# An adaLN attention block on one core: the third tile's mean on two engines, and the shift in two column halves

## The chip, the core and the metric

The kernel runs on one core of a Trainium2 chip. A core has a matrix engine (TensorE, PE in the profile; its weight loads are the row PEld), a vector engine (VectorE, DVE), a scalar engine (ScalarE, ACT), a general engine (GpSimd, POOL) and a sync engine (SyncE, SP) that here issues nearly all DMA transfers. Each engine works through its own queue of instructions in order, and waits on semaphores for the others. Working data lie in SBUF, results of matrix products in the eight banks of PSUM. The metric is the device time of one execution in microseconds, the median of several runs.

## The reference

```python
B, N, D = (2, 256, 1152)
mod = (_silu(c) @ w_mod).reshape(B, 6, 1, D)
shift_a, scale_a, gate_a, shift_m, scale_m, gate_m = [mod[:, i] for i in range(6)]
h = _layernorm(x, axis=-1) * (1 + scale_a) + shift_a
qkv = h @ wqkv
q, k, v = (qkv[..., :D].copy(), qkv[..., D:2 * D].copy(), qkv[..., 2 * D:].copy())
p = _softmax(jnp.einsum('bqd,bkd->bqk', q, k) * D ** (-0.5), axis=-1)
a = jnp.einsum('bqk,bkd->bqd', p, v) @ wo
return x + gate_a * a
```

All inputs are bf16. wqkv is 1152 x 3456, wo 1152 x 1152, w_mod 1152 x 6912, of which only the columns of shift_a, scale_a and gate_a are used.

## The kernel before, in words

The 512 tokens (two batches of 256) are four token tiles of 128; the width of 1152 is nine blocks of 128. `tok(b)` is a batch's tokens, `one(t)` a tile's. Every instruction is recorded by a helper class, so all of them have line 85 in the profile, and `pin` (line 98) fixes each engine's order to the order of the program text. The order of the text is therefore the schedule of every queue, SP's loads among them.

**Loads.** SP issues x's tiles 0 to 2, the columns of `scale_a` for blocks 0 and 1 (`load_s(PA, ...)`), K's first row of weight blocks (`load_k(0, 1)`), x's tile 3 (line 175), K's second row (line 176), and then the other scale columns in parts PB, PC, PD (blocks 2 to 4, 5 and 6, 7 and 8) between K's rows. Behind K come the columns of `shift_a` into wH (line 190, three loads by rows), Q's rows (line 192), the gate's columns into wG (lines 542 to 545), V and wo.

**The start.** Eleven matmuls on junk data keep PE going (`fillers`, line 362). A token tile's mean is formed by DVE statistics (tile 0), by an ACT pass with an accumulated sum (tiles 1 and 2, `act_mean`), or by ACT over 640 columns and DVE over 512, the two sums joined on DVE (tile 3, lines 402 to 405). `centre` subtracts it on DVE (xc), PE transposes the nine blocks (tp in PSUM), and DVE and ACT copy them to xcT. The division by the standard deviation comes later (`normalised`, with rstd spread over the tokens).

**Scale.** For blocks 0 and 1, `scale_open` writes ones into a bank with a one-row matmul, and `scale_rows` adds the product of silu(c) and the weights, so the bank holds 1 + scale. For PB, `scale_tiles` (line 297) computes the product in four column groups of PE side by side, with 32 rows of output each, and `scale_turned` transposes 32 x 32 squares on DVE into sT and adds 1 into s1p. `scaled` and `scaled_tp` multiply xcT or tp by it: hTs, the input of K.

**K.** Five of K's nine column blocks accumulate in five banks (`accs`) over the nine rows: `k_part` for rows 0 and 1, batch 0, tile 2 and tile 3 apart, since they arrive apart; `k_step` for the other rows with all 512 tokens. The remaining four column blocks are done for rows 0 and 1 in pairs (`pair_part`, bank psE), put away in `held` (`park`), and finished later by `held_block` (bank psK) with `add_held`. PSUM is five banks in a ring (MM) and three single ones (BA, BB, BC); a new use of a bank waits until its last reader is done.

**Shift.** `shift_tiles` (line 502) multiplies silu(c) by wH, in four column groups again, into psH; `shift_turned` transposes it to shT, and `shifted(i)` adds it to hT, block by block and batch by batch, every third on ACT. Then nine rows of Q follow (five accumulators, then four more blocks), then scores, V, attention times V, and wo with the gate. The gate is formed on DVE meanwhile, in 18 multiply-adds over wG's rows (`gate_steps`), and summed over partitions on POOL.

Of the kernel before, what the change touches and what calls it, by code (L numbers as in the profile page):

```python
# [16 lines left out]
def kernel(  # L17
# [10 lines left out]
    P = 128  # L28
# [37 lines left out]
    def bank(shape, name, dtype=None, where=None):  # L66
        if where is None:
            where = ring[turn_no[0] % len(ring)]
            turn_no[0] += 1
        return where[0].tile(shape, dtype or F32, tag=where[1], name=name)  # L70
# [36 lines left out]
    def tok(b):  # L107
        return slice(b * N, (b + 1) * N)

    def one(t):  # L110
        return slice(t * P, (t + 1) * P)
# [25 lines left out]
    ones_row = const.tile([1, 2 * NR], BF16)  # L137
# [10 lines left out]
    def load_x(t):  # L148
        spq.dma_start(out=x_sb[:, t, :], in_=x_f[t * P : (t + 1) * P, :])

    def load_mod(tile_, which, k0, k1, c0, c1):
        spq.dma_start(out=tile_[:, k0:k1, c0:c1], in_=wmod_v[:, k0:k1, which, c0:c1])
# [4 lines left out]
    def load_k(k0, k1, c0=0, c1=D):  # L157
        spq.dma_start(out=wK[:, k0:k1, c0:c1], in_=wqkv_v[:, k0:k1, D + c0 : D + c1])

    def load_q(k0, k1):  # L160
        spq.dma_start(out=wQ[:, k0:k1, :], in_=wqkv_v[:, k0:k1, 0:D])
# [12 lines left out]
    load_k(0, 1)  # L174
    load_x(3)
    load_k(1, 2)
# [12 lines left out]
    for k0, k1 in ((0, 4), (4, 8), (8, KT)):  # L189
        load_mod(wH, 0, k0, k1, 0, D)  # L190
    for k0, k1 in ((0, 1), (1, 3), (3, 5), (5, 7)):
        load_q(k0, k1)

# [28 lines left out]
    ssum3 = small.tile([P, 1], F32, tag="ssum", name="ssum")  # L222
# [12 lines left out]
    def act_mean(t):  # L235
        sca.activation(out=xc[:, t, :], in_=x_sb[:, t, :], func=ACT.Copy, scale=-1.0 / D,
                       accum_out=nmean[:, t : t + 1])

# [4 lines left out]
    def centre(t, scalar, op, c0=0, c1=D):  # L243
        vec.tensor_scalar(out=xc[:, t, c0:c1], in0=x_sb[:, t, c0:c1], scalar1=scalar, scalar2=None, op0=op)
# [4 lines left out]
    def transposes(t, h, where):  # L249
        k0, k1 = HALF[h]  # L250
        tp = bank([P, 5, P], "tp", BF16, where)
        for k in range(k0, k1):
            ten.transpose(tp[:, k - k0, :], xc[:, t, k * P : (k + 1) * P], ident)
        tps[t, h] = tp

    def xcT_copy(t, h, on_dve, skip=0):
        k0, k1 = HALF[h]
        dst, srct = xcT[:, k0 + skip : k1, one(t)], tps[t, h][:, skip : k1 - k0, :]
        if on_dve:
            vec.tensor_copy(out=dst, in_=srct)  # L260
        else:
            sca.copy(out=dst, in_=srct)

# [33 lines left out]
    def scale_tiles(part, where):  # L297
        psS[part] = bank([P, part[1] - part[0], 32], "psS", where=where)
        for kk in range(KT):
            for j in range(4):  # L300
                ten.matmul(psS[part][32 * j : 32 * j + 32], lhsT=sc_rhs(kk), rhs=wS_v[:, kk, part[0] : part[1], j, :],
                           start=(kk == 0), stop=(kk == KT - 1))

    def scale_turned(part):
        vec.transpose(out=sT[:, part[0] : part[1], :].rearrange("p k c -> p (k c)"),
                      in_=psS[part].rearrange("p k c -> p (k c)"))
        vec.tensor_scalar_add(out=s1p[:, part[0] : part[1], :], in0=sT[:, part[0] : part[1], 0:B], scalar1=1.0)

    def scaled(k, sl, scalar):
        vec.tensor_scalar(out=hTs[:, k, sl], in0=xcT[:, k, sl], scalar1=scalar, scalar2=None, op0=ALU.mult)  # L310

    def scaled_tp(k, t):
        vec.tensor_scalar(out=hTs[:, k, one(t)], in0=tps[t, 0][:, k, :], scalar1=s1p[:, k, t // NQ : t // NQ + 1],
                          scalar2=None, op0=ALU.mult)

    def scaled_b(k, b):
        scaled(k, tok(b), s1p[:, k, b : b + 1])
# [52 lines left out]
    act_mean(2)  # L370
    gps.tensor_scalar_mul(out=snm[:, 1:3], in0=nmean[:, 1:3], scalar1=float(D) ** -0.5)
    transposes(0, 0, MM)
    transposes(0, 1, MM)
    xcT_copy(0, 0, True)
    xcT_copy(0, 1, False)
    transposes(1, 0, MM)
    transposes(1, 1, MM)
    scale_rows(PA, 0, 4)
    xcT_copy(1, 0, True)
    centre(2, nmean[:, 2:3], ALU.add)  # L380
    xcT_copy(1, 1, False)
    scale_rows(PA, 4, KT, js=[(0, 1), (1, 2)])
    scaled(0, tok(0), psS[PA][:, 0, 0:1])
    vec.tensor_copy(out=s1p[:, PA[0] : PA[1], :], in_=psS[PA][:, :, 0:B])
    transposes(2, 0, BB)
    transposes(2, 1, BC)
    scaled_tp(0, 2)
    scaled_b(1, 0)
    scaled_tp(1, 2)
    xcT_copy(2, 0, True, skip=KA)  # L390
    xcT_copy(2, 1, False)
# [3 lines left out]
    k_part(0, tok(0))  # L395
    k_part(0, one(2))
    pr20 = pair(1, 0, BA)
    pair_part(pr20, 0)
    pr10 = pair(0, 0, BC)
    pair_part(pr10, 0)  # L400
    H3, C3 = 5 * P, 4 * P
    sca.activation(out=xc[:, 3, 0:H3], in_=x_sb[:, 3, 0:H3], func=ACT.Copy, accum_out=ssum3)
    half3 = small.tile([P, 1], F32, tag="half3", name="half3")
    vec.reduce_sum(out=half3, in_=x_sb[:, 3, H3:D], axis=AX.X)
    vec.tensor_scalar(out=nmean[:, 3:4], in0=half3, scalar1=ssum3, scalar2=-1.0 / D, op0=ALU.add, op1=ALU.mult)
    centre(3, nmean[:, 3:4], ALU.add, 0, C3)
    centre(3, nmean[:, 3:4], ALU.add, C3, D)
    pair_part(pr10, 1)
    k_part(1, tok(0))
    k_part(1, one(2))  # L410
    park(pr10)
    transposes(3, 0, BB)
    pair_part(pr20, 1)
    transposes(3, 1, BC)
    scaled_tp(0, 3)
    scaled_tp(1, 3)
    xcT_copy(3, 0, True, skip=KA)
    park(pr20)
# [4 lines left out]
    k_part(0, one(3))  # L423
    scale_tiles(PB, BB)
    k_part(1, one(3))
    scale_turned(PB)
    for k in range(*PB):
        for b in range(B):
            scaled_b(k, b)
# [35 lines left out]
    held_block(1, PB, BC)  # L465
    pT3 = bank([P, P], "pT3", BF16, BB)
# [3 lines left out]
    k_step(5)  # L470
# [28 lines left out]
    psH = bank([P, KT, 32], "psH", where=BA)  # L499
    wH_v = wH.rearrange("p kk (k j c) -> p kk k j c", k=KT, j=4)  # L500

    def shift_tiles(kk0, kk1):
        for kk in range(kk0, kk1):
            for j in range(4):
                ten.matmul(psH[32 * j : 32 * j + 32], lhsT=sc_rhs(kk), rhs=wH_v[:, kk, :, j, :],
                           start=(kk == 0), stop=(kk == KT - 1))

    held_block(3, (KA, KA + 2), BC)
    shift_tiles(0, KT)
# [3 lines left out]
    def shift_turned(k0, k1):  # L513
        vec.transpose(out=shT[:, k0:k1, :].rearrange("p k c -> p (k c)"),
                      in_=psH[:, k0:k1, :].rearrange("p k c -> p (k c)"))
# [10 lines left out]
    shift_turned(0, 3)  # L526
    for i in range(KT * B):
        if i == B:
            shift_turned(3, KT)
        if i in (3 * B, 5 * B):  # L530
            normalised(KT - 2 if i == 3 * B else KT - 1)
        shifted(i)
    for i in (2, 3):
        add_held(i)
# [7 lines left out]
    load_mod(wG, 2, 0, 3, 0, D)  # L542
    load_q(7, KT)
    load_mod(wG, 2, 3, 6, 0, D)
    load_mod(wG, 2, 6, KT, 0, D)
# [6 lines left out]
    gates = [(b, kt) for g in range(0, KT, 3) for b in range(B) for kt in range(g, g + 3)]  # L552
# [15 lines left out]
    for k in range(KT):  # L568
        for f in range(QACC):
            ten.matmul(q_acc[f], lhsT=wq(k, f), rhs=hT[:, k, :], start=(k == 0), stop=(k == KT - 1))  # L570
# [177 lines left out]
```

## Time and profile before

The median of three runs is 95.64 us (95.59 to 95.98).

| | |
|---|---|
| profiled execution, its own time | 95.63 us |
| its span in the profile | 93.9 us |
| PE busy | 89.2 us, 95% of the span, 664 matmuls |
| DVE busy | 69.6 us, 74% |
| ACT busy | 33.9 us, 36% |
| POOL busy | 20.8 us, 22% |
| granted TensorE clock | 1.00 |
| read from HBM | 19.76 MB |
| first transposes / first K product / first Q product start | 6.47 / 8.95 / 30.26 us |

Times in the timelines count from the span's start. "x36" is the number of instructions in a line, and the duration ahead of it runs from the start of the first to the modelled end of the last. A matmul's end is modelled, so one can begin before the one ahead of it has ended. What stands in brackets is idle time of the engine before the line and what ended it. `SPq` lines are the issues of DMA transfers; the last number of a line in the list of transfers is the time from issue to landing.

### The profile page before, as it was taken

How to read it: one execution, taken by the hardware profiler on the slowest of the kernel's cores; microseconds unless marked ns; L12 is line 12 of the kernel's file. 1: busy time of each engine (PE TensorE's matmuls, PEld its weight loads, DVE VectorE, ACT ScalarE, POOL GpSimd, SP SyncE). 2: the span in 40 equal slices, each digit the busy share in tenths (PEclk: the TensorE clock that was granted, in tenths of full speed). 3: DMA queues.
4: the chain of work that ended last, by engine and by line, in shares of the span. 5: the costliest groups of instructions: out<-in, count | busy, mean ns of one | idle time of the engine just before them, and what ended most of it. 6: DMA issues, size and time to landing. Idle time of an engine off the chain costs nothing.

```text
span 93.9 us, 1692 instructions
## 1 busy us (share of the span) xinstructions
PE 89.2 (95%) x664; PEld 52.8 (56%) x664; DVE 69.6 (74%) x134; ACT 33.9 (36%) x69; POOL 20.8 (22%) x26
## 2 busy tenths in 40 slices
PE   3999999999999999999999999999999999999970
PEld 1348884545445444444478665656578665665660
DVE  2478789245997977999999899990028587888880
ACT  5188788002643600284220687324246200000010
POOL 5623000800000000000000000008999990002000
PEclk9999999999999999999999999999999999999999
DMA  2999999999999999999999702200000000312212
GB/s 23 345 282 374 372 397 362 369 410 407 407 405 410 414 408 412 402 373 365 381 407 410 296 17 56 63 0 0 0 0 0 0 0 8 125 42 83 114 45 92
DMA packets 17232, 21.31 MB, mean 227 GB/s; under 512 B 2249, under 2 KB 10569, under 8 KB 17225
## 3 DMA queue, kind: packets, MB, share of 16 engines
q1 hardware_dynamic: 16809, 21.17, 62.3%
q8 instruction: 5, 0.08, 0.3%
q10 hardware_dynamic: 416, 0.04, 0.3%
q14 instruction: 2, 0.02, 0.0%
HBM read 19.76 MB, written 1.18 MB: 223 GB/s over the span
## 4 chain that ended last, share of the span: by engine, by line
PE 91%; DVE 4%; issue 1%
PE ps L85 39%; PE psQ L85 19%; PE acc L85 11%; PE psK L85 7%; PE junk_ps L85 5%; PE s_ps L85 4%; PE tp L85 2%; PE psE L85 2%; PE psS L85 2%; DVE o_sb L85 2%; DVE ga L85 2%; PE psH L85 1%; DVE xc L85 1%; DVE junk L85 1%; PE bc_ps L85 0%
## 5 line engine op out<-in xcount | busy, mean ns | idle before, releaser
L85 POOL PARTITION_ALL_REDUCE gate_bc<-gacc x2 | 13.7, 6886 | 44.6 <-DVE gacc L85 44.6
L85 DVE SCALAR_TENSOR_TENSOR gacc<-wG,scT_f,gacc 128x1152 f32<-128x1152 bf16 x16 | 22.4, 1416 | 0.4
L85 PE MATMUL ps<-wV,hT 128*128 128x384 bf16 x108 | 17.7, 326 | 0.0
L85 PE MATMUL psQ<-hT,wQ 128*128 128x512 bf16 x81 | 17.6, 379 | 0.0
L85 PE MATMUL ps<-wO,attnT 128*128 128x384 bf16 (+3 forms) x108 | 17.2, 322 | 0.0
L85 PEld LDWEIGHTS <-attnT 128*128 128x128 bf16 x117 | 11.1, 98 | 6.5
L85 PEld LDWEIGHTS <-hT 128*128 128x128 bf16 x108 | 10.6, 98 | 6.9
L85 PEld LDWEIGHTS <-wK 128*128 128x128 bf16 x109 | 9.5, 97 | 6.9 <-issue 0.2
L85 PEld LDWEIGHTS <-wQ 128*128 128x128 bf16 x81 | 7.9, 98 | 9.6
L85 PE MATMUL acc<-hTs,wK 128*128 128x512 bf16 (+2 forms) x65 | 11.2, 314 | 0.0
L85 DVE TENSOR_TENSOR ga<-ps,gate_bc 128x384 f32<-128x384 f32 (+3 forms) x12 | 6.5, 545 | 3.0 <-PE ps L85 3.0
L85 ACT CAST qkT<-psQ 128x512 bf16<-128x512 f32 x9 | 4.9, 597 | 10.6 <-PE psQ L85 10.6
L85 DVE CAST attnT<-ps 128x512 bf16<-128x512 f32 (+1 forms) x6 | 3.5, 603 | 6.8 <-PE ps L85 6.8
L85 ACT CAST v_sb<-ps 128x384 bf16<-128x384 f32 x12 | 5.5, 476 | 7.9 <-PE ps L85 7.9
L85 PE MATMUL psK<-hTs,wK 128*128 128x512 bf16 x28 | 7.0, 379 | 0.0
L85 DVE TENSOR_TENSOR o_sb<-ga,x_sb 128x384 bf16<-128x384 f32 (+3 forms) x12 | 6.6, 548 | 0.4
L85 ACT CAST o_sb<-ps 128x128 bf16<-128x128 f32 x1 | 0.3, 265 | 17.3 <-PE ps L85 17.3
L85 PE MATMUL junk_ps<-junk 128*128 128x512 bf16 x11 | 4.9, 629 | 1.5 <-DVE junk L85 1.5
L85 DVE TENSOR_TENSOR hT<-hTs,held 128x512 bf16<-128x512 bf16 x9 | 5.8, 688 | 0.4 <-ACT held L85 0.4
L85 DVE BATCH_NORM_STATS2 stats<-x_sb 128x6 f32<-128x384 bf16 x6 | 3.1, 544 | 2.3 <-DMA x_sb<-in_x_dram 2.3
L85 PEld LDWEIGHTS <-junk 128*128 128x128 bf16 (+1 forms) x13 | 1.6, 134 | 5.0 <-issue 3.4
L85 PE MATMUL s_ps<-qkT 128*128 128x256 bf16 x36 | 4.1, 273 | 0.0
(81 smaller groups left out, 84.2 us busy)
## 6 DMA issues: line engine op xcount, KB each, us to landing
wG<-in_w_mod_dram SPq DMA_DIRECT2D x3, 864.0 KB, 12.5
wV<-in_wqkv_dram SPq DMA_DIRECT2D x3, 864.0 KB, 13.4
wO<-in_wo_dram SPq DMA_DIRECT2D x3, 864.0 KB, 9.0
wH<-in_w_mod_dram SPq DMA_DIRECT2D x2, 1152.0 KB, 9.3
wQ<-in_wqkv_dram SPq DMA_DIRECT2D x4, 576.0 KB, 11.7
wK<-in_wqkv_dram SPq DMA_DIRECT2D x7, 288.0 KB, 7.0
wS<-in_w_mod_dram SPq DMA_DIRECT2D x3, 320.0 KB, 6.3
x_sb<-in_x_dram SPq DMA_DIRECT2D x3, 288.0 KB, 3.4
```

Source lines behind the costliest of these rows:

```text
L85: r = fn(*a, **k)
```

## The change

- **Tile 2's mean** is formed as tile 3's was, by a common function `shared_mean`: ACT sums 640 columns, DVE 512, and DVE centres the two parts.
- **Transposes of tiles 0 and 1** (`transposes_apart`): blocks 0 and 1 of both tiles go to one PSUM bank, from which `scaled_firsts` makes hTs directly, 256 tokens at a time; the other seven blocks of a tile go to a bank of their own, and ACT copies them to xcT. Tile 2's first eight blocks share a bank, the ninth has another.
- **Order of K's start:** the k_parts and pairs of rows 0 and 1 for tiles 0 to 2 all stand ahead of tile 3's transposes, and both k_parts of tile 3 ahead of the scale of PB.
- **Scale of PB:** the bank is opened with ones, so sT holds 1 + scale and is used as it is.
- **K's second row** is loaded in two pieces, 640 columns ahead of x's tile 3 and 512 behind it.
- **Shift** is computed in two column halves, HA (blocks 0 to 4) where the whole stood, HB (blocks 5 to 8) ahead of the fifth row of Q. wH is loaded in the same halves, HB behind Q's first five rows.
- **Gate:** wG's three loads and the gate's order change from rows 3, 3, 3 to 2, 3, 4. The transpose of rstd's parts (pT3) stands behind K's sixth row instead of ahead of it.

```diff
--- before.py
+++ after.py
@@ -134,7 +134,7 @@
 
     c_sb = const.tile([P, B, KT], BF16)
     x_sb = act.tile([P, TT, D], BF16)
-    ones_row = const.tile([1, 2 * NR], BF16)
+    ones_row = const.tile([1, (PB[1] - PB[0]) * NR], BF16)
     gps.memset(ones_row, 1.0)
     sca.preload_act_table_set("natural_log_exp_and_others")
     sca.dma_start(out=c_sb, in_=c.rearrange("b (p k) -> p b k", k=KT))
@@ -172,8 +172,9 @@
     load_s(PA, 0, 4)
     load_s(PA, 4, KT)
     load_k(0, 1)
+    load_k(1, 2, 0, NACC * P)
     load_x(3)
-    load_k(1, 2)
+    load_k(1, 2, NACC * P, D)
     load_s(PB, 0, 4)
     load_s(PB, 4, KT)
     load_k(2, 3)
@@ -186,10 +187,12 @@
     load_s(PD, 4, KT)
     load_k(6, 7)
     load_k(7, KT)
-    for k0, k1 in ((0, 4), (4, 8), (8, KT)):
-        load_mod(wH, 0, k0, k1, 0, D)
-    for k0, k1 in ((0, 1), (1, 3), (3, 5), (5, 7)):
+    HA, HB = (0, 5), (5, KT)
+    load_mod(wH, 0, 0, KT, HA[0] * P, HA[1] * P)
+    for k0, k1 in ((0, 1), (1, 3), (3, 5)):
         load_q(k0, k1)
+    load_mod(wH, 0, 0, KT, HB[0] * P, HB[1] * P)
+    load_q(5, 7)
 
     junk_ps = bank([P, 512], "junk_ps", where=BB)
 
@@ -219,7 +222,6 @@
     nmean = const.tile([P, TT], F32)
     xc = act.tile([P, TT, D], BF16, tag="a1")
     xcT = act.tile([P, KT, T], BF16, tag="a2")
-    ssum3 = small.tile([P, 1], F32, tag="ssum", name="ssum")
 
     def bn_part(t, st, s):
         vec.bn_stats(out=st[:, s, :], in_=x_sb[:, t, s * CW : (s + 1) * CW])
@@ -236,6 +238,18 @@
         sca.activation(out=xc[:, t, :], in_=x_sb[:, t, :], func=ACT.Copy, scale=-1.0 / D,
                        accum_out=nmean[:, t : t + 1])
 
+    SPLIT, C_FIRST = 5 * P, 4 * P
+
+    def shared_mean(t):
+        half_a = small.tile([P, 1], F32, tag="half_a", name="half_a")
+        half_v = small.tile([P, 1], F32, tag="half_v", name="half_v")
+        sca.activation(out=xc[:, t, 0:SPLIT], in_=x_sb[:, t, 0:SPLIT], func=ACT.Copy, accum_out=half_a)
+        vec.reduce_sum(out=half_v, in_=x_sb[:, t, SPLIT:D], axis=AX.X)
+        vec.tensor_scalar(out=nmean[:, t : t + 1], in0=half_v, scalar1=half_a, scalar2=-1.0 / D,
+                          op0=ALU.add, op1=ALU.mult)
+        for c0, c1 in ((0, C_FIRST), (C_FIRST, D)):
+            centre(t, nmean[:, t : t + 1], ALU.add, c0, c1)
+
     def act_var(t):
         sca.activation(out=xc[:, t, :], in_=x_sb[:, t, :], func=ACT.Square, bias=snm[:, t : t + 1],
                        scale=float(D) ** -0.5, accum_out=mvs[:, t, 1:2])
@@ -260,6 +274,19 @@
             vec.tensor_copy(out=dst, in_=srct)
         else:
             sca.copy(out=dst, in_=srct)
+
+
+    firsts = {}
+
+    def transposes_apart(t, where):
+        if not firsts:
+            firsts["tp"] = bank([P, KA, NQ, P], "tp", BF16, MM)
+        rest_tp = bank([P, KT - KA, P], "tp", BF16, where)
+        for k in range(KA):
+            ten.transpose(firsts["tp"][:, k, t, :], xc[:, t, k * P : (k + 1) * P], ident)
+        for k in range(KA, KT):
+            ten.transpose(rest_tp[:, k - KA, :], xc[:, t, k * P : (k + 1) * P], ident)
+        sca.copy(out=xcT[:, KA:KT, one(t)], in_=rest_tp)
 
     s1p = const.tile([P, KT, B], F32)
     hTs = act.tile([P, KT, T], BF16, tag="a3")
@@ -294,20 +321,22 @@
     wS_v = wS.rearrange("p kk (k j c) -> p kk k j c", k=KT, j=4)
     sT = const.tile([P, KT, 32], F32)
 
-    def scale_tiles(part, where):
-        psS[part] = bank([P, part[1] - part[0], 32], "psS", where=where)
+    def scale_tiles(part):
         for kk in range(KT):
             for j in range(4):
                 ten.matmul(psS[part][32 * j : 32 * j + 32], lhsT=sc_rhs(kk), rhs=wS_v[:, kk, part[0] : part[1], j, :],
-                           start=(kk == 0), stop=(kk == KT - 1))
+                           start=False, stop=(kk == KT - 1), skip_group_check=True)
 
     def scale_turned(part):
         vec.transpose(out=sT[:, part[0] : part[1], :].rearrange("p k c -> p (k c)"),
                       in_=psS[part].rearrange("p k c -> p (k c)"))
-        vec.tensor_scalar_add(out=s1p[:, part[0] : part[1], :], in0=sT[:, part[0] : part[1], 0:B], scalar1=1.0)
 
     def scaled(k, sl, scalar):
         vec.tensor_scalar(out=hTs[:, k, sl], in0=xcT[:, k, sl], scalar1=scalar, scalar2=None, op0=ALU.mult)
+
+    def scaled_firsts(k, scalar):
+        vec.tensor_scalar(out=hTs[:, k, tok(0)], in0=firsts["tp"][:, k].rearrange("p t c -> p (t c)"), scalar1=scalar,
+                          scalar2=None, op0=ALU.mult)
 
     def scaled_tp(k, t):
         vec.tensor_scalar(out=hTs[:, k, one(t)], in0=tps[t, 0][:, k, :], scalar1=s1p[:, k, t // NQ : t // NQ + 1],
@@ -367,66 +396,56 @@
     centre(0, mvs[:, 0, 0:1], ALU.subtract)
     act_mean(1)
     centre(1, nmean[:, 1:2], ALU.add)
-    act_mean(2)
+    shared_mean(2)
     gps.tensor_scalar_mul(out=snm[:, 1:3], in0=nmean[:, 1:3], scalar1=float(D) ** -0.5)
-    transposes(0, 0, MM)
-    transposes(0, 1, MM)
-    xcT_copy(0, 0, True)
-    xcT_copy(0, 1, False)
-    transposes(1, 0, MM)
-    transposes(1, 1, MM)
+    transposes_apart(0, MM)
+    transposes_apart(1, BC)
     scale_rows(PA, 0, 4)
-    xcT_copy(1, 0, True)
-    centre(2, nmean[:, 2:3], ALU.add)
-    xcT_copy(1, 1, False)
     scale_rows(PA, 4, KT, js=[(0, 1), (1, 2)])
-    scaled(0, tok(0), psS[PA][:, 0, 0:1])
+    scaled_firsts(0, psS[PA][:, 0, 0:1])
     vec.tensor_copy(out=s1p[:, PA[0] : PA[1], :], in_=psS[PA][:, :, 0:B])
-    transposes(2, 0, BB)
-    transposes(2, 1, BC)
-    scaled_tp(0, 2)
-    scaled_b(1, 0)
-    scaled_tp(1, 2)
-    xcT_copy(2, 0, True, skip=KA)
-    xcT_copy(2, 1, False)
+    scaled_firsts(1, s1p[:, 1, 0:1])
+    tps[2, 0] = bank([P, KT - 1, P], "tp", BF16, BB)
+    tps[2, 1] = bank([P, 1, P], "tp", BF16, BA)
+    for k in range(KT):
+        ten.transpose(tps[2, 0][:, k, :] if k < KT - 1 else tps[2, 1][:, 0, :], xc[:, 2, k * P : (k + 1) * P], ident)
+    for k in range(KA):
+        scaled_tp(k, 2)
+    vec.tensor_copy(out=xcT[:, KA : KT - 1, one(2)], in_=tps[2, 0][:, KA:, :])
+    sca.copy(out=xcT[:, KT - 1, one(2)], in_=tps[2, 1][:, 0, :])
 
 
     accs = [bank([P, T], "acc", where=MM) for _ in range(NACC)]
     k_part(0, tok(0))
+    pr10 = pair(0, 0, BC)
+    pair_part(pr10, 0)
     k_part(0, one(2))
     pr20 = pair(1, 0, BA)
     pair_part(pr20, 0)
-    pr10 = pair(0, 0, BC)
-    pair_part(pr10, 0)
-    H3, C3 = 5 * P, 4 * P
-    sca.activation(out=xc[:, 3, 0:H3], in_=x_sb[:, 3, 0:H3], func=ACT.Copy, accum_out=ssum3)
-    half3 = small.tile([P, 1], F32, tag="half3", name="half3")
-    vec.reduce_sum(out=half3, in_=x_sb[:, 3, H3:D], axis=AX.X)
-    vec.tensor_scalar(out=nmean[:, 3:4], in0=half3, scalar1=ssum3, scalar2=-1.0 / D, op0=ALU.add, op1=ALU.mult)
-    centre(3, nmean[:, 3:4], ALU.add, 0, C3)
-    centre(3, nmean[:, 3:4], ALU.add, C3, D)
-    pair_part(pr10, 1)
+    shared_mean(3)
     k_part(1, tok(0))
     k_part(1, one(2))
+    pair_part(pr10, 1)
     park(pr10)
+    pair_part(pr20, 1)
     transposes(3, 0, BB)
-    pair_part(pr20, 1)
     transposes(3, 1, BC)
     scaled_tp(0, 3)
     scaled_tp(1, 3)
+    park(pr20)
     xcT_copy(3, 0, True, skip=KA)
-    park(pr20)
     xcT_copy(3, 1, False)
     st3 = small.tile([P, NCH, 6], F32, tag="stats", name="stats")
     bn_part(3, st3, 0)
     act_var(1)
-    k_part(0, one(3))
-    scale_tiles(PB, BB)
-    k_part(1, one(3))
+    for k in range(KA):
+        k_part(k, one(3))
+    scale_open(PB, BB)
+    scale_tiles(PB)
     scale_turned(PB)
     for k in range(*PB):
         for b in range(B):
-            scaled_b(k, b)
+            scaled(k, tok(b), sT[:, k, b : b + 1])
     bn_part(3, st3, 1)
     bn_part(3, st3, 2)
     vec.bn_aggr(out=mvs[:, 3, :], in_=st3)
@@ -463,11 +482,11 @@
     scale_part(PC)
     held_block(0, (4, 5))
     held_block(1, PB, BC)
+    k_step(5)
     pT3 = bank([P, P], "pT3", BF16, BB)
     ten.transpose(pT3, parts_sq, ident)
     masked = const.tile([P, TT, P], BF16)
     vec.tensor_tensor(out=masked, in0=pT3.unsqueeze(1).to_broadcast([P, TT, P]), in1=mask, op=ALU.mult)
-    k_step(5)
     held_block(0, (5, 6))
     held_block(1, (5, 6))
     k_step(6, 0, 2)
@@ -496,23 +515,24 @@
     held_block(2, (KA, KT), BB)
 
 
-    psH = bank([P, KT, 32], "psH", where=BA)
+    psH = {}
     wH_v = wH.rearrange("p kk (k j c) -> p kk k j c", k=KT, j=4)
 
-    def shift_tiles(kk0, kk1):
-        for kk in range(kk0, kk1):
+    def shift_tiles(part):
+        psH[part] = bank([P, part[1] - part[0], 32], "psH", where=BA)
+        for kk in range(KT):
             for j in range(4):
-                ten.matmul(psH[32 * j : 32 * j + 32], lhsT=sc_rhs(kk), rhs=wH_v[:, kk, :, j, :],
+                ten.matmul(psH[part][32 * j : 32 * j + 32], lhsT=sc_rhs(kk), rhs=wH_v[:, kk, part[0] : part[1], j, :],
                            start=(kk == 0), stop=(kk == KT - 1))
 
     held_block(3, (KA, KA + 2), BC)
-    shift_tiles(0, KT)
+    shift_tiles(HA)
     held_block(3, (KA + 2, KT))
     shT = const.tile([P, KT, 32], F32)
 
-    def shift_turned(k0, k1):
+    def shift_turned(part, k0, k1):
         vec.transpose(out=shT[:, k0:k1, :].rearrange("p k c -> p (k c)"),
-                      in_=psH[:, k0:k1, :].rearrange("p k c -> p (k c)"))
+                      in_=psH[part][:, k0 - part[0] : k1 - part[0], :].rearrange("p k c -> p (k c)"))
 
     def shifted(i):
         k, b = divmod(i, B)
@@ -523,13 +543,13 @@
             vec.tensor_scalar(out=hT[:, k, tok(b)], in0=hT[:, k, tok(b)], scalar1=shT[:, k, b : b + 1],
                               scalar2=None, op0=ALU.add)
 
-    shift_turned(0, 3)
-    for i in range(KT * B):
+    shift_turned(HA, 0, 3)
+    for i in range(HA[1] * B):
         if i == B:
-            shift_turned(3, KT)
-        if i in (3 * B, 5 * B):
-            normalised(KT - 2 if i == 3 * B else KT - 1)
+            shift_turned(HA, 3, HA[1])
         shifted(i)
+    normalised(KT - 2)
+    normalised(KT - 1)
     for i in (2, 3):
         add_held(i)
 
@@ -539,17 +559,18 @@
 
     wG = wmpool.tile([P, KT, D], BF16, tag="wS")
     wO = wmpool.tile([P, KT, D], BF16, tag="wH")
-    load_mod(wG, 2, 0, 3, 0, D)
+    GROUPS = ((0, 2), (2, 5), (5, KT))
+    load_mod(wG, 2, 0, 2, 0, D)
     load_q(7, KT)
-    load_mod(wG, 2, 3, 6, 0, D)
-    load_mod(wG, 2, 6, KT, 0, D)
+    for k0, k1 in GROUPS[1:]:
+        load_mod(wG, 2, k0, k1, 0, D)
     for i in range(NCH):
         load_v(i)
     for k0 in range(0, KT, 3):
         spq.dma_start(out=wO[:, k0 : k0 + 3, :], in_=wo_v[:, k0 : k0 + 3, :])
 
     gacc = act.tile([P, B, D], F32, tag="a3")
-    gates = [(b, kt) for g in range(0, KT, 3) for b in range(B) for kt in range(g, g + 3)]
+    gates = [(b, kt) for g in GROUPS for b in range(B) for kt in range(*g)]
 
     def gate_steps(n):
         for _ in range(n):
@@ -566,6 +587,11 @@
     QACC = 5
     q_acc = [bank([P, T], "psQ", where=MM) for _ in range(QACC)]
     for k in range(KT):
+        if k == HA[1] - 1:
+            shift_tiles(HB)
+            shift_turned(HB, *HB)
+            for i in range(HB[0] * B, HB[1] * B):
+                shifted(i)
         for f in range(QACC):
             ten.matmul(q_acc[f], lhsT=wq(k, f), rhs=hT[:, k, :], start=(k == 0), stop=(k == KT - 1))
     for f in range(QACC):
```

## The prediction

> **What bounds the kernel now.** I read the page first, then the chain in order of time, then a table of windows and the timelines of the stretches in which the chain leaves PE. The page's slices (tenths of busy PE) and the table (per window: length, then PE, PEld, DVE, ACT, POOL busy):
>
> ```profile
> PE   3999999999999999999999999999999999999970
> ...
> 8.44:14.17 5.73, 5.73 (x101) 5.07 (x101) 4.65 (x19) 4.52 (x8) 0.08 (x1) 1.00 1.06 384
> 14.17:30.26 16.09, 16.09 (x139) 7.98 (x137) 11.28 (x32) 5.74 (x13) 2.30 (x7) 1.00 1.07 396
> 30.26:47.90 17.64, 17.64 (x84) 8.06 (x83) 16.44 (x25) 6.26 (x13) 0.00 (x0) 1.00 1.06 394
> ```
>
> PE is the bound, and the columns behind POOL (clock 1.00, DMA share 1.06, GB/s) show the DMA queues full beside it. Busy hides small gaps, since a matmul's modelled end lies 0.16 us behind the next start. So I count starts: 512 columns every 0.2155 us (81 psQ in 17.46 us), 256 every 0.108, 128 every 0.055. From 14.17 to 30.26 the work by these prices (63 x 0.2155, two psS of 0.44, pT, bc_ps, psH) is 16.0 of 16.09: nothing to win there, nor in Q. The chain names the stretch with gaps:
>
> ```profile
> 7.59 0.28 issue
> 7.87 0.52 DVE xc L85
> 8.39 0.05 issue
> 8.44 0.68 PE tp L85 x9
> ...
> 11.42 0.32 PE tp L85 x4
> ...
> 14.32 3.24 PE acc L85 x15
> ```
>
> PE waits for the centred third tile, 8.05 to 8.44 (0.39), and small gaps follow: 0.14 ahead of psS at 7.60, 0.10 ahead of the fourth tile's transposes (they start at 11.35), 0.05 at 12.11. All that can be won is 0.68 us. The PE timeline around the two stages computed in narrow 128*32 tiles, which the change touches:
>
> ```profile
> 12.50 0.57 PE L85 MATMUL psS<-wS,scT_rep 128*32 128x96 bf16 x36
> 13.00 0.45 PE L85 MATMUL acc<-hTs,wK 128*128 128x128 bf16 x5
> 13.29 1.04 PE L85 MATMUL psE<-hTs,wK 128*128 128x256 bf16 x8
> 14.17 0.38 PE L85 MATMUL acc<-hTs,wK 128*128 128x512 bf16 x1
> 27.95 1.29 PE L85 MATMUL psH<-wH,scT_rep 128*32 128x288 bf16 x36
> 29.17 0.39 PE L85 MATMUL psK<-hTs,wK 128*128 128x512 bf16 x1
> ```
>
> Four narrow tiles run together: psH takes 0.123 a group of four (288 columns), nine groups 1.11; psS 0.040 (96 columns), 0.36. What is left is the change of tile shape: 0.09 into psH (27.86 to 27.95), 0.11 out, 0.13 out of psS (12.87 to 13.00). Last, DVE's timeline, and the landing times of three loads issued at 3.56, 4.12 and 4.66:
>
> ```profile
> 10.60 0.21 DVE L85 TENSOR_SCALAR nmean<-half,ssum 128x1 f32<-128x1 f32 x1 [0.27 <-ACT xc L85]
> 10.85 0.65 DVE L85 TENSOR_SCALAR xc<-x_sb,nmean 128x512 bf16<-128x512 bf16 x2
> 11.77 0.47 DVE L85 TENSOR_SCALAR hTs<-tp,s1p 128x128 bf16<-128x128 bf16 x2 [0.27 <-PE tp L85]
> ...
> 13.12 0.28 DVE L85 STREAM_TRANSPOSE sT<-psS 128x96 f32<-128x96 f32 x1 [0.21 <-PE psS L85]
> 13.44 0.16 DVE L85 TENSOR_SCALAR s1p<-sT 128x6 f32<-128x6 f32 x1
> ```
> ```profile
> wK<-in_wqkv_dram SPq DMA_DIRECT2D x1, 288.0 KB, 4.8
> ```
> ```profile
> x_sb<-in_x_dram SPq DMA_DIRECT2D x1, 288.0 KB, 5.2
> ```
> ```profile
> wK<-in_wqkv_dram SPq DMA_DIRECT2D x1, 288.0 KB, 5.5
> ```
>
> K's first row lands at 8.36, the fourth tile of x at 9.32, K's second row at 10.16: 0.84 to 0.96 us per 288 KB, one behind the other.
>
> **Third tile and first blocks.** ACT's mean over 640 columns (0.74, read-out to +0.83, as the fourth tile's) runs from x's arrival at 6.35 to 7.18, DVE's sum (0.67) from 6.48 to 7.15, nmean at 7.21, the halves centred 7.46 to 7.81 and 7.73 to 8.11. On DVE this stands ahead of the first scalings, where two copies of 0.42 are gone. PE transposes tile 3 from 8.05; its last block uses psS's old bank and waits for the s1p copy: scaled block 0 at 8.04 (0.31), s1p to 8.45, so the block goes at 8.51. K's product starts at 8.57, not 8.95: 0.38 early. Its fourth and fifth accumulators take the banks of the first blocks (scaled by 8.77) and of the first rest copy (ACT, 896 columns, 0.91 by the slope from 0.27 for 128 to 0.69 for 640, done 8.13): ready. The next reuse, pr10's, waits for the second rest copy, 8.93, against 9.11. Then 2.50 us of PE work in the new order (1.08 + 0.55 in k_parts, 0.87 in pairs) ends at 11.07.
>
> **Fourth tile.** In the new load order 160 KB of K's second row go ahead of x's fourth tile. No row has that piece: between 0 and 0.84 us, the whole row's price; by size 0.5. So x lands at 9.82 instead of 9.32; SP's extra issue (0.4) hides in the 5.2 us from issue to landing, and K's second half still lands near 10.2, needed at 10.63. Before, engines and not x set the start (ACT free at 9.74). Now ACT is free at 9.1 and DVE at 9.6, so x does: ACT 9.84, nmean +0.86, centring +0.25, transposes +0.50, at 11.42 to 11.45 against 11.35. The 0.38 us turns into PE idle from 11.07. Cost +0.08, bounds -0.28 (PE's own arrival) to +0.42.
>
> **From there to the third k step.** Before: 2.82 us (11.35 to 14.17), with one pair of 0.22 laid under the wait for the scaled blocks and psS ahead of the second k_part. Now the pair is used up before, and both k_parts stand ahead of psS. Scaled blocks at +0.42, k_parts from +0.76 to +1.31, then the opening matmul (one row, 96 columns) and psS. scale_open's row before shows 0.16 from its start to the next and 0.12 ahead of it; so psS starts at +1.59, its last group at +1.91; DVE's transpose comes 0.26 later as before (12.86 to 13.12), +2.18, the scalings at +2.50 (the s1p add, 0.19, is what the opening saves), two of them end at +2.98, k_step 2 at +3.05. PE itself would be there at +2.94. Cost +0.23; if the opening's shape changes cost nothing, -0.05.
>
> **Shift in halves.** HA and HB have 160 and 128 columns: nine groups at 66.7 and 53.3 ns (the row's 0.123 for 288, scaled), 0.60 + 0.48 against 1.11: -0.03. A second entry and exit costs 0.09 + 0.11. Sum +0.17, bounds 0 to +0.3. What covers the new wait: after HB, DVE's transpose at +0.3 from the last matmul, 0.28, then the add on ACT (0.51, row 0) makes hT's block 5 ready at about +1.18, against PE's next need at 0.11 + five matmuls, 1.08 + 0.03: a slack of 0.05, so bounds 0 to 0.15, taken as 0. DVE's queue: HB's transpose waits for PE at 35.8, and behind it stand five adds (0.21 each) and the gates, which start at 37.3 instead of 35.70. Scores move from 50.01 to 51.6, the probability transposes' end from 60.6 to 62.2 (needed at 69.2), the all-reduces' end from 77.3 to 78.9 (needed at 81.73), POOL's wo_last from 85.5 to 87.1 (needed at 90.28): covered. Loads: HA lands about 3 us before 28.46 (wH's last), HB, behind five rows of Q, near 32.2, needed at 35.1; Q's last two rows come behind a smaller gate load, earlier than 37.04. pT's place behind k_step 5, the gate groups and the ones row on POOL: 0, since PE is dense there, and POOL's parts (19.01) are then 1 us early.
>
> The narrow halves are where a rule speaks. The psS row starts its 36 matmuls 10 ns apart. The Trainium skill, "TensorE: Matmul & The Clock Gate", section "Wait — 56ns, not 53.3ns?", says that starts never come closer than about 25 ns however few the columns are; here the trace differs. By that rule 72 narrow matmuls would take 1.8 us, and the sum would end near 96.8; by the row it stays.
>
> **Sum.** 0.08 + 0.23 + 0.17 = +0.48 on the profiled execution's 95.63 us (span 93.9 and 1.73 around it, 0.01 under the median of 95.64): 96.1.
>
> **Rivals.**
> - Third tile's gain survives, not slower: x lands by 9.45, 1.62 before PE's arrival at 11.07. For it: the 288 KB ahead of x may have cost more than its bytes; against: the landings follow the bytes. 95.63 - 0.28 + 0.23 + 0.17 = 95.75. It decides from a landing before about 9.8: every tenth is a tenth.
> - DMA and Q stall: the two halves of K's row cost as much as a row each, x lands at 10.1 (+0.28), and hT's block 5 is late (+0.15): 96.5. For it: the slack of 0.05; against: bytes.
> - Narrow matmuls paced by count: the 18 psS of 32 columns at 17.83 start 25 ns apart; 72 so paced cost 1.84 against 1.11, +0.76 over my -0.03: 96.9. Against: psS's 36.
> - All gaps close and the shape changes hide: 95.63 - 0.68: 95.0. Against: x's landing, and the 0.11 out of psH.
>
> **Chances.** Forecast 0.60 (95.8 to 96.4), gain survives 0.20, stalls 0.14, paced 0.02, all gaps 0.04. A measurement here tells 0.5%, 0.48 us, from no change; my forecast lies on that edge, so half of it is slower: slower 0.30 + 0.14 + 0.02 = 0.46, same 0.30 + 0.20 = 0.50, faster 0.04. Range 95.6 to 96.6: the forecast, the surviving gain and most of the stalls.
>
> **What would show it.** K's first product near 8.57; PE idle of some 0.35 ahead of tile 4's transposes, with x landing near 9.8; the third k step near 14.5; psH in two groups of 0.60 and 0.48 with gaps of 0.1; Q without a wait at its sixth row; the rest shifted by 0.5. Wrong if x lands at 9.4, if the one-row opening leaves no gap, or if the gates' delay shows at the end.

## The result and the profile after

The changed kernel takes 96.50 us (median of six runs, 96.13 to 96.65); the kernel before, run beside it, 95.65 us. The ratio is 1.007, with a 95% interval of 1.0045 to 1.0095: slower by 0.7%. Its profiled execution took 96.59 us, its span is 94.8 us.

Four starts of PE are enough to say where the time went. They are read from the PE timelines: K's first product, the fourth tile's transposes, the third k step (the first matmul with all 512 tokens), and the first scores.

| us | K's first product | tile 4's transposes | third k step | first scores | last two apart |
|---|---|---|---|---|---|
| before | 8.95 | 11.35 | 14.17 | 47.74 | 33.57 |
| forecast | 8.57 | 11.43 | 14.5 | 48.2 | 33.74 |
| changed | 9.09 | 11.65 | 14.78 | 48.65 | 33.87 |

Behind the scores the two executions take the same (94.8 - 48.65 = 46.15 and 93.9 - 47.74 = 46.16). So 0.61 us are lost up to the third k step and 0.30 behind it. The chain of the changed kernel, in order of time (start, length, what):

```profile
7.90 0.61 PE psS L85 x18
8.52 0.03 issue
8.54 0.35 DVE hTs L85
8.90 0.08 DVE s1p L85
8.98 0.05 issue
9.02 0.23 PE tp L85
9.25 0.55 PE acc L85 x5
...
11.34 0.23 PE psE L85 x2
11.57 0.02 issue
11.59 0.59 ACT held L85
12.19 0.04 issue
12.23 0.44 PE tp L85 x5
...
14.85 3.33 PE acc L85 x15
```

Before, this chain left PE once in this stretch, for DVE's copy and centring of the third tile (7.52 to 8.39). That wait is gone, and two others stand in its place. The third tile's last block waits for the first scaling, which waits for psS (8.52 to 9.02). The PE lines of psS, before and changed, and the DVE line of the scaling in the changed kernel:

```profile
7.60 0.61 PE L85 MATMUL psS<-scT_rep,wS 128*128 128x32 bf16 x18
```
```profile
7.74 0.76 PE L85 MATMUL psS<-scT_rep,wS 128*128 128x32 bf16 x18
```
```profile
8.54 0.35 DVE L85 TENSOR_SCALAR hTs<-tp,psS 128x256 bf16<-128x256 bf16 x1 [0.48 <-PE psS L85]
```

psS starts 0.14 us later than before, and it stops in the middle for the second scale columns, which landed at 8.0 instead of 7.6; that is another 0.15. So it ends at 8.50 instead of 8.21. The second wait: between the two parts of tile 4's transposes PE waits for ACT's copy of the first pair (held, 11.59), because the second part goes into that pair's bank. The PE timeline of the second half of this stretch, and of the second shift half:

```profile
12.23 0.44 PE L85 MATMUL tp<-ident,xc 128*128 128x128 bf16 x5 [0.20 <-ACT held L85]
12.51 0.72 PE L85 MATMUL acc<-hTs,wK 128*128 128x128 bf16 x10
13.16 0.21 PE L85 MATMUL psS<-ones_row,junk 1*128 1x96 bf16 x1
13.30 0.57 PE L85 MATMUL psS<-wS,scT_rep 128*32 128x96 bf16 x36
13.80 1.05 PE L85 MATMUL psE<-hTs,wK 128*128 128x256 bf16 x8
...
34.86 0.69 PE L85 MATMUL psH<-wH,scT_rep 128*32 128x128 bf16 x36
35.48 0.39 PE L85 MATMUL psQ<-hT,wQ 128*128 128x512 bf16 x1
```

The one-row opening costs its gaps: the last k_part matmul starts at 13.01, so the next could start at 13.07; the opening starts at 13.16, 0.09 later, and the narrow tiles at 13.30. The second shift half holds PE from 34.76 (0.2155 behind the start of the last matmul of Q's fourth row, 34.55) to 35.48.

The starts differ from one execution to the next by as much as the change moves them. So in what follows a part is measured between two starts of one profiled execution; medians of whole runs of variants 0.2 to 0.3 us apart are given, but do not order them.

### The profile page after: what moved, and what is told of

It is laid out like the page before. It is cut to its first block, busy times and chain, and to the rows that moved or that the text cites. A ratio compares the mean times of both kernels' runs of the same rounds, so it can differ in the third digit from the quotient of the medians.

```text
span 94.8 us, 1766 instructions
## 1 busy us (share of the span) xinstructions
PE 90.1 (95%) x701; PEld 53.3 (56%) x701; DVE 70.3 (74%) x135; ACT 33.6 (35%) x69; POOL 20.7 (22%) x26
## 4 chain that ended last, share of the span: by engine, by line
PE 91%; DVE 4%; ACT 1%; issue 0%
PE ps L85 38%; PE psQ L85 19%; PE acc L85 10%; PE psK L85 6%; PE junk_ps L85 5%; PE s_ps L85 4%; PE psS L85 2%; PE tp L85 2%; PE psE L85 2%; DVE o_sb L85 2%; DVE ga L85 2%; PE psH L85 1%; ACT held L85 1%; DVE junk L85 1%; DVE hTs L85 0%
## 5 line engine op out<-in xcount | busy, mean ns | idle before, releaser
L85 ACT ACTIVATE hT<-hT,shT 128x256 bf16<-128x256 bf16 x6 | 2.6, 498 | 7.0 <-DVE shT L85 7.0
```

Source lines behind the costliest of these rows:

```text
L85: r = fn(*a, **k)
```

## The experiments

All profiled executions, and the median of the runs where there were several (the kernel before, beside them, 95.66 to 95.67, and 95.94 for the last three):

| kernel | K's first product | tile 4's transposes | third k step | first scores | last two apart | median |
|---|---|---|---|---|---|---|
| before_again | 8.96 | 11.36 | 14.18 | 47.75 | 33.57 | |
| before_third | 9.78 | 12.18 | 14.99 | 48.57 | 33.58 | |
| after_again | 9.02 | 11.58 | 14.71 | 48.58 | 33.87 | |
| x_first | 9.09 | 11.62 | 14.78 | 48.66 | 33.88 | 96.21 |
| shift_whole | 8.72 | 11.29 | 14.41 | 48.04 | 33.63 | 96.20 |
| pair_early | 8.68 | 11.44 | 14.47 | 48.34 | 33.87 | 96.63 |
| pb_plain | 8.57 | 11.48 | 14.55 | 48.43 | 33.88 | 96.37 |
| fillers_9 | 8.74 | 11.73 | 14.75 | 48.62 | 33.87 | 96.32 |
| best_a | 8.91 | 11.55 | 14.51 | 48.14 | 33.63 | 96.06 |
| halves_alone | 9.28 | 11.68 | 14.49 | 48.31 | 33.82 | 96.12 |
| early_alone | 8.55 | 11.29 | 14.12 | 47.92 | 33.80 | 95.86 |

**The changed kernel and the kernel before once more**, no edit.

> The changed kernel once more, unaltered. Theory A (the start differs from execution to execution): the second half of the first scale columns lands anywhere from 7.6 to 8.1 us, and the whole stands 0.4 us lower when it lands early, near 96.15. Theory B (the new load order delays these columns): they land at 8.0 again and K's first product starts at 9.1 again.

> The kernel before once more, unaltered. Theory A: its first scale columns land between 7.6 and 8.1 us in one execution or another, and where they land late its time is near 96.0. Theory B: they land at 7.6 and K's first product starts at 8.95 again.

before_again took 95.65 us, with the scale columns at 7.6 and K's first product at 8.96, as its theory B has it; late columns did not occur. after_again took 96.48 us. The second scale columns landed at 7.5 this time (issued at 3.01, 4.5 us), and K's first product still came at 9.02: neither theory. What both executions of the changed kernel have in common is the pace of the first transposes. The PE timelines up to 6.95 us of the kernel before, of the changed one, and of shift_whole:

```profile
6.47 0.68 PE L85 MATMUL tp<-ident,xc 128*128 128x128 bf16 x7
```
```profile
6.47 0.71 PE L85 MATMUL tp<-ident,xc 128*128 128x128 bf16 x5
```
```profile
6.29 0.84 PE L85 MATMUL tp<-ident,xc 128*128 128x128 bf16 x12 [0.27 <-DVE xc L85]
```

Where the first transposes start 0.107 us apart, PE runs at half its pace, and so it does in the junk matmuls ahead of them (0.427 apart, against 0.2155 for the same shape later). The matmul behind the eleven then starts at 6.31, behind the first centred tile (6.14 before, 5.99 changed). Where PE was up to pace sooner, the first transposes wait for DVE, and K's first product comes at 8.55 to 8.74, except where a load was late (x_first and best_a, below).

The Trainium skill, "TensorE: Matmul & The Clock Gate", section "Part 1: The HAM clock gate", says that PE runs at half clock until about 3.4 us of steady work, in a window that runs free, so that the moment differs from run to run; the transposes' 0.107 and 0.055 agree. The profile's clock reads 1.00 throughout all the same, because it counts time for which the trace has no clock record as full speed. The trace's first record, at full speed, begins at 6.76 us in the kernel before, at 7.04 and 7.23 in the two executions of the changed kernel and at 5.25 in shift_whole, and there the starts pass from the slow distance to the quick one. (In pair_early, pb_plain and fillers_9 the trace has no such record.)

The kernel before starts nearly as slowly in its first two executions (seven transposes by 6.95, five in the changed kernel). There psS ends at 8.21, and the third tile's transposes wait for DVE until 8.44, so some 0.2 us of delay in psS (an estimate from these two numbers) would not show. In the changed kernel this wait is gone, and psS itself holds the first scaling, for 0.48 us, and for 0.22 in after_again, where the scale columns were early and the pace alone was late. In the quick executions DVE does not wait for psS at all. How much of the slow pace the kernel before takes up is not shown; its DVE timeline speaks against all of it:

```profile
7.02 0.93 DVE L85 COPY xcT<-tp 128x512 bf16<-128x512 bf16 x2 [0.45 <-PE tp L85]
7.87 0.51 DVE L85 TENSOR_SCALAR xc<-x_sb,nmean 128x1152 bf16<-128x1152 bf16 x1
```

DVE waits for the first transposes, copies them, and only then centres the third tile, whose mean ACT had ready at 7.60. So a quicker PE could bring that centring forward too.

**x's fourth tile first.**

```diff
-    load_k(1, 2, 0, NACC * P)
     load_x(3)
+    load_k(1, 2, 0, NACC * P)
```

> The changed kernel with x's fourth tile loaded ahead of both pieces of K's second row. If x's landing sets the fourth tile's transposes: x lands 0.5 us earlier (9.4), the transposes start when PE arrives (11.1 to 11.6), and the third k step comes up to 0.3 us earlier. Rival: PE's own arrival sets them, and then nothing moves, or the k_part of row 1 waits for its weights, which land 0.5 us later.

x landed at 9.7 (4.12 + 5.6), not at 9.4, and the third k step stayed at 14.78. Here K's first row landed late, at 9.0 (issued at 3.56, 5.5 us), and PE's arrival set tile 4. Its PE timeline:

```profile
9.09 0.72 PE L85 MATMUL acc<-hTs,wK 128*128 128x256 bf16 x5 [0.26 <-DMA wK<-in_wqkv_dram]
...
12.24 0.44 PE L85 MATMUL tp<-ident,xc 128*128 128x128 bf16 x5 [0.23 <-ACT held L85]
```

The rival held, for a reason that neither had: another load. Its median is 0.29 lower than the changed kernel's, but the intervals of the two ratios to the kernel before overlap (1.0030 to 1.0080, against 1.0045 to 1.0095), so that it is faster is not shown.

**The shift undivided.** wH is loaded in three parts by rows ahead of Q, and `shift_tiles` runs once over all nine blocks, as before; the last two `normalised` steps go back into its loop.

```diff
-    HA, HB = (0, 5), (5, KT)
+    HA = (0, KT)
...
-        if k == HA[1] - 1:
-            shift_tiles(HB)
...
```

> The changed kernel with the shift undivided, and its weights loaded whole ahead of Q, as before. Theory: the second entry into and exit from the narrow tiles goes away, so 0.24 us less than the changed kernel, with the start as late as there. Rival: the halves cost nothing in themselves, and the whole shift, reached 0.6 us later, gives the same time.

From the third k step to the scores 33.63 us instead of 33.87: the 0.24 of the theory. Behind the scores this execution took 46.30 us instead of 46.16, as best_a below did; PE's part is the same there, the last output landed 0.08 later, and the reason stays open. So the whole time shows only part of the 0.24. The other way round, on the kernel before (the same edit reversed):

> The kernel before with the shift and its weights in two column halves, and nothing else of the change. Theory: from the third k step to the first scores 0.24 us more (33.8 instead of 33.57), near 95.9. Rival: the halves cost only where the start is late, and the time stays at 95.65.

33.82 instead of 33.57, +0.25 (its median 96.12 against 95.94, ratio 1.0022, interval 0.9993 to 1.0051, too wide for that size). The PE timeline of halves_alone, where the third k step starts at 14.49 because x's second tile came late:

```profile
28.28 0.81 PE L85 MATMUL psH<-wH,scT_rep 128*32 128x160 bf16 x36
29.02 1.25 PE L85 MATMUL psK<-hTs,wK 128*128 128x512 bf16 x5
...
48.31 4.09 PE L85 MATMUL s_ps<-qkT 128*128 128x256 bf16 x36
```

The first half takes 0.74 to the next start (1.22 for the whole shift before), the second, in the changed kernel, 0.62 and 0.10 of entry: 0.24 more in all, and no wait behind it.

**The first pair early**, so that its bank is free for tile 4.

```diff
+    pair_part(pr10, 1)
     k_part(1, tok(0))
     k_part(1, one(2))
-    pair_part(pr10, 1)
```

> The changed kernel with the first pair's second half, and so the copy that frees its bank, put ahead of the k_parts of row 1. Theory: the second part of tile 4's transposes waits for that bank (0.36 us of idle PE); without the wait it starts 0.3 us earlier against K's first product (+2.8 instead of +3.14 us), and the third k step comes at +5.4 instead of +5.69. Rival (x's landing sets tile 4): the first part of the transposes stays where it is and the third k step moves by less than 0.1.

The wait is gone: nine transposes in one piece. Its PE timeline, and its weight loads:

```profile
8.68 0.71 PE L85 MATMUL acc<-hTs,wK 128*128 128x256 bf16 x5
...
11.44 0.67 PE L85 MATMUL tp<-ident,xc 128*128 128x128 bf16 x9
12.20 0.72 PE L85 MATMUL acc<-hTs,wK 128*128 128x128 bf16 x10
...
14.47 1.46 PE L85 MATMUL acc<-hTs,wK 128*128 128x512 bf16 x6
```
```profile
10.16 1.16 PEld L85 LDWEIGHTS <-wK 128*128 128x128 bf16 x14 [0.34 <-DMA wK<-in_wqkv_dram]
```

But against K's first product the third k step came at +5.79, not +5.4. K's product was early here, and the pair that now stands ahead needs the second piece of K's second row, which landed at 10.1: PE stood 0.22 us for it and then ran without a gap to tile 4, at 11.44. x's landing (4.69 + 5.1 = 9.8) would have allowed the transposes at about the same time (an estimate: in pb_plain below x landed at 9.8 too, and they waited until 11.48). From there it takes 3.03 us, against 3.13 in the changed kernel. So there are limits close together, x's landing, K's second row and PE's arrival with the pair's bank behind it, and taking one away uncovers the next.

**PB's scale without the one-row opening.**

```diff
-    scale_open(PB, BB)
+    psS[PB] = bank([P, PB[1] - PB[0], 32], "psS", where=BB)
...
+        vec.tensor_scalar_add(out=s1p[:, part[0] : part[1], :], in0=sT[:, part[0] : part[1], 0:B], scalar1=1.0)
...
```

> The changed kernel with PB's scale computed as before, without the one-row matmul, and one added on DVE. Prediction's terms: PE saves 0.24 us ahead of the narrow tiles, DVE pays 0.19, so the third k step comes 0.05 earlier. Rival: the opening leaves no gap of its own, then it comes 0.1 to 0.2 later.

From tile 4's transposes to the third k step 3.07 us, against 3.03 in pair_early, where no bank wait disturbs either. So without the opening the third k step comes 0.04 later, not 0.05 earlier as the terms had it, and less late than the rival: the opening is worth its gaps. DVE pays the 0.19, but PE saves only 0.15 and not 0.24, since entering the narrow tiles from the full shape has a gap of 0.09 of its own. This execution also has the forecast's K product to the hundredth, and still took 96.33 us; its PE timeline:

```profile
8.57 0.71 PE L85 MATMUL acc<-hTs,wK 128*128 128x256 bf16 x5
...
11.48 0.68 PE L85 MATMUL tp<-ident,xc 128*128 128x128 bf16 x9 [0.22 <-DVE xc L85]
...
14.55 1.24 PE L85 MATMUL acc<-hTs,wK 128*128 128x512 bf16 x5
```

PE stands idle ahead of tile 4 (its four pair matmuls of 0.108 from 10.66 on are through at 11.09) and waits for the centred tile, whose x landed at 9.8.

**Nine junk matmuls instead of eleven.**

```diff
-    fillers(11)
+    fillers(9)
```

> The changed kernel with nine junk matmuls at the start instead of eleven. Theory: where PE's clock is still slow the eleven end at 6.31 us, behind the first centred tile (6.1), and the changed start, which has no wait for DVE left, hands that on; with nine the first transposes start at 6.2 and K's first product at about 8.8 instead of 9.05. Rival: the second scale columns' landing (7.5 to 8.0) sets K's first product and it stays at 9.05.

K's first product came at 8.74, but the junk matmuls had picked up pace by themselves (they ended by 5.2 us, so the eleven would not have been late either), and x landed at 10.1. Inconclusive: the execution that would tell was not caught.

**Four edits together.** The undivided shift and the first pair early, as above; the order of before around tile 4; tile 4's sum ahead of tile 3's copy on DVE.

```diff
-    pair_part(pr20, 1)
     transposes(3, 0, BB)
+    pair_part(pr20, 1)
     transposes(3, 1, BC)
...
-    for k in range(KA):
-        k_part(k, one(3))
+    k_part(0, one(3))
     scale_open(PB, BB)
     scale_tiles(PB)
+    k_part(1, one(3))
```

> The changed kernel with the shift undivided, the first pair's second half early, the order of before around tile 4 (second pair between its transposes, PB's scale ahead of the second k_part), and tile 4's sum ahead of tile 3's copy on DVE. By the parts: shift -0.24, tile 4 and PB -0.45, so 95.75, level with the kernel before. Rival: x's landing at 9.7 then bounds tile 4's transposes at 11.3 and only 0.3 of the 0.69 is won, near 96.1.

96.06 us, ratio 1.0038 (1.0017 to 1.0059): the rival's time. Its PE timeline shows a load at the first place, the scale columns, and DVE at the second; the DVE timeline stands below it:

```profile
7.90 0.41 PE L85 MATMUL psS<-scT_rep,wS 128*128 128x32 bf16 x10 [0.38 <-DMA wS<-in_w_mod_dram]
...
11.55 0.38 PE L85 MATMUL tp<-ident,xc 128*128 128x128 bf16 x4 [0.17 <-DVE xc L85]
```
```profile
9.74 0.69 DVE L85 TENSOR_REDUCE half_v<-x_sb 128x1 f32<-128x512 bf16 x1 [0.18 <-DMA x_sb<-in_x_dram]
10.34 0.55 DVE L85 COPY xcT<-tp 128x768 bf16<-128x768 bf16 x1
10.81 0.20 DVE L85 TENSOR_SCALAR nmean<-half_v,half_a 128x1 f32<-128x1 f32 x1
```

x landed at 9.7, as the rival says, but tile 4 came at 11.55 and not at 11.3. Tile 3's copy, which the last of the four edits puts behind tile 4's sum, holds nmean until 10.81, though ACT's sum was read out at 10.57. So the rival's time was met, and its cause only in part.

**The new start alone**, with the load order, the shift, the PB scale and the order around tile 4 of the kernel before, and the first pair early. The gate's groups and the place of pT3 stay as in the changed kernel.

> The kernel before with the changed start alone (tile 3's mean on two engines, first blocks scaled from one bank, the first pair's second half early), and its own load order, shift, PB scale and order around tile 4. Theory: K's first product comes 0.2 to 0.4 us earlier, and the loads then set the pace: K's second row lands at 10.2, so row 1 ends at 11.2 and the third k step comes at 14.0 to 14.1 instead of 14.17; 0.1 to 0.2 us less than the kernel before, near 95.5. Rival: the whole 0.38 us arrives (95.3), or the two extra banks' waits make it no faster than the kernel before.

95.86 us against 95.94, ratio 1.0006 (0.9978 to 1.0035): no change. K's first product came 0.40 earlier than in the kernel before (8.55), and the third k step 0.05 earlier. Its PE timeline, and its weight loads (PEld):

```profile
10.24 0.39 PE L85 MATMUL psE<-hTs,wK 128*128 128x256 bf16 x2 [0.26 <-DMA wK<-in_wqkv_dram]
...
14.12 3.40 PE L85 MATMUL acc<-hTs,wK 128*128 128x512 bf16 x15
```
```profile
20.88 0.11 PEld L85 LDWEIGHTS <-wK 128*128 128x128 bf16 x2 [0.49 <-DMA wK<-in_wqkv_dram]
```

K's second row landed at 10.2 and held PE; then another K row held it at 20.88, and 0.17 us were lost once more (33.80 instead of 33.63). In this execution, what PE gained at the start, the loads took back.

**The kernel before a third time.**

> The kernel before once more. If PE's clock happens to have risen early in this execution (junk matmuls ended by 5.6 us), the first transposes start at 6.2 and K's first product near 8.7 instead of 8.95, and the time is near 95.4; if not, it repeats 95.65. Rival: K's first product waits for DVE either way and stays at 8.95.

Neither: x's second tile landed at 6.0 instead of 4.65, ACT's mean waited for it, and everything stood 0.82 later, at 96.52 us. Its ACT timeline:

```profile
6.06 1.16 ACT L85 ACTIVATE xc<-x_sb 128x1152 bf16<-128x1152 bf16 x1 [1.89 <-DMA x_sb<-in_x_dram]
```

So an execution of the kernel before with a quick PE start was not seen in a profile.

## Why the prediction was right or wrong

- **The direction, and the time within its range.** 96.1 was forecast, on the edge of what can be told from no change, and 96.50 measured: the slower side of the edge, 0.4 above the number, inside 95.6 to 96.6.
- **K's first product at 8.57: right where PE was quick, wrong for the changed kernel's own executions.** 8.55 and 8.57 were met with a quick PE; the changed kernel gave 9.09 and 9.02. DVE's part held: the third tile was centred by 8.06 (forecast 8.11). The step that failed is "scaled block 0 at 8.04". It follows DVE's queue alone and leaves out the product psS that the block is multiplied by. The working's own row of the kernel before has psS from 7.60 to 8.21, so 8.25 was the earliest there, and K's product some 0.2 later than forecast (an estimate from that row). The other 0.3 of the 0.5 is psS ending at 8.50: a clock that rose at 7.04 instead of 6.76 (0.14) and the late scale columns (0.15). For the same reason PE transposes tile 3 from 8.35, not 8.05. The working named no cover for either. The "0.14 ahead of psS at 7.60", read as a gap that could be won, is the same slow clock: the transposes ahead of it start 0.107 apart at first. Of the 0.5, 0.3 arrives at the third k step.
- **Tile 4 bound by x's landing: the landing was right, that it binds was half right.** Forecast 9.82; 9.9 and 9.8 in the changed kernel's two executions, 9.7 to 10.1 in all seven with this load order. It sets tile 4 in pb_plain and fillers_9 (11.48 and 11.73, PE idle ahead; forecast 11.42 to 11.45); in the changed execution PE itself arrived as late, at 11.61, and tile 4 started at 11.65. The rival "gain survives" fell: x never landed by 9.45 in this load order.
- **From there to the third k step, +3.05: measured 3.13**, 3.03 without the bank wait. That wait, tile 4's second part on the first pair's copy, was not in the working; it lies mostly under the wait for the scaled blocks, and costs 0.1.
- **The opening, 0.12 ahead of it, 0.16 to the next start, and 0.19 saved on DVE: nearly right.** 0.09 and 0.14 on PE. Its balance is a gain of 0.04, since the plain narrow tiles have an entry of 0.09 as well.
- **Shift halves, +0.17: measured +0.24 to +0.25.** Mis-sized by 0.07: with what the sum counts of entry and exit the halves take 0.74 and 0.72 us, not 0.71 and 0.68. Most of it is the price of a group of four, 69 and 56 ns (574 and 467 ns from a half's first start to its last), not 66.7 and 53.3; the row's 0.123, scaled by columns, would have been 68 and 55. Another 0.06 lies between the third k step and the scores even with the undivided shift (33.63 against 33.57). It is pT3's move, which the working put at 0 because PE is dense there: ahead of k_step 5 PE waits for a scaled block from DVE, and that matmul starts 5.04 us behind the third k step in both kernels. Before, pT stood in this wait of 0.06 and cost nothing; now the wait is empty, and pT costs 0.06 behind the step. The cover of the new wait held: Q runs on without one, and the second half's weights are there in time.
- **Gates and all-reduces: right.** The gates started at 36.93 (forecast 37.3), the scores' first DVE step moved from 50.01 to 51.11 (forecast 51.6), and behind the first scores nothing is longer.
- **The rival of matmuls paced by count fell.** 72 narrow matmuls took 1.36 us to the next starts (0.74 + 0.62), less than the 1.84 it priced them at. The floor of 25 ns between starts in the Trainium skill, "TensorE: Matmul & The Clock Gate", section "Wait — 56ns, not 53.3ns?", does not hold in narrow tiles: the 36 of the second half start within 0.47 us. The stalls' rival described the sum (96.5) but not its cause: hT's block 5 was in time.
- **What the start alone explains.** pb_plain has the forecast's K product and took 96.33 us, so about half of the 0.4 is left without the late start: the shift's 0.07, pT3's 0.06, and a few hundredths up to the third k step.

## What to carry to other kernels

Before a wait is taken away, list what it covers: a slow clock at the start, loads that land a few tenths apart from run to run, a product that ends just ahead of it, a bank that is freed late; the price of the edit is what comes through when the cover is gone. Where DMA queues are full, a smaller piece moved ahead delays what stands behind it by about its bytes (x landed 1.5 us behind K's first row, on average over seven executions, with the 160 KB piece between them, and 0.9 over six without), and PE time won ahead of a load can be given back at that load. A narrow stage cut in two pays its shape changes twice, here 0.24 us, of which the rows of before gave 0.17. A small instruction that fills a wait is free only where it stands.

## What the runs showed of the hardware

- A load's time from issue to landing differs between executions of the same program by more than the effects studied: in the three of the kernel before the second scale columns took 4.6, 4.6 and 5.6 us and x's second tile 3.4, 3.4 and 4.8; over all thirteen profiled executions they took 4.3 to 5.6 and 3.1 to 4.8.
- PE's pace at the start differs too: the matmul behind the same eleven junk matmuls starts at 5.4 to 6.3 us. In the ten executions that have a clock record, full speed begins 2.9 to 5.8 us behind the first junk matmul (1.50). The profile's mean clock of 1.00 does not show it; the distances of starts do.
- Narrow 128*32 matmuls of 96 columns started 10 ns apart on average, of 128 columns 13 ns (36 within 0.47 us): the four of a group 3 to 4 ns apart, one group of 128 columns 56 ns behind the other. Each change between the narrow, the one-row and the full shape cost 0.09 to 0.14 us.
